# A Fourier mixing layer and a SwiGLU block on one core: value weights issued one fold earlier, row clears behind the rows, an angle counter in PSUM, Wo in longer packets

## The chip, the cores and the metric

The kernel runs on 1 core of one Trainium2 chip. The metric is device time in microseconds. Five engines take part: TensorE (PE, with its weight loads as PEld), VectorE (DVE), ScalarE (ACT), GpSimd (POOL) and SyncE (SP). SP issues nothing but DMAs; ACT and POOL issue some too, between their instructions. Each engine runs its instructions in the order in which they stand, and waits on semaphores for the others.

## The reference

```
def _attn_ref(x):                      # x: 8 x 3008 x 256, f32
    X = np.fft.fft(x, axis=1)
    X = np.fft.fft(X, axis=2)
    return X.real
def _moe_ref(x, w_gate, w_val, w_out): # x: 24064 x 256, d_ff = 1536
    g = x @ w_gate
    silu = g * (1.0 / (1.0 + np.exp(-g)))
    val = x @ w_val
    return silu * val @ w_out
```

The second takes the first's output as its rows. All inputs and the output are f32.

## The kernel before

**What is computed how.** The Fourier transform along 256 is folded into the gate and value weights: they are multiplied by tables of cosines (`CD`) and sines (`SDt`) once and give `Wp`, `Wq` and `Wm` (`Wq` with mirrored signs), three bf16 tiles of 128 rows, for gate and value (`gv`) 1536 columns each. The transform along 3008 is done by symmetry: rows of x are folded into sums and differences (on POOL, `fold_steps`), and tables `Tab` of cosines and sines times these give `Pt` (from the cosines) and `Qt` (from the sines), 512 columns of outputs a tile, for a plus and a mirrored minus half. For each tile and each of 12 chunks of d_ff, PE multiplies `Wp` with `Pt` and `Wq` or `Wm` with `Qt` (line 1086), ACT takes the silu (1167, 1199, 1210), DVE or POOL multiply by the value half (1191, 1217, 1187, 1230) and give `hp` and `hm`, and PE multiplies these with `Wo` (1257). Chunk f of d_ff is the columns f*128 to f*128+127 of the weights and row block f of `Wo`.

**Two parts.** The prologue (to line 748) is written out by hand: batch 0's rows, the tables, the first weights. What comes after stands in an order that a planner (`Sched`, line 860) makes from estimated costs and a table of shifts while the program is built; it also gives each product a PSUM bank (`bank`, line 1090). Its order is fixed in the program; nothing is decided on the chip.

**The prologue's steps around the change.** x is loaded into `XA` (128 rows by 8 blocks; batch 0's first rows) and `XC0` (the rest of batch 0) by `rise_c`, `fall_a` and `fall_c` on the queues of SP and ACT. `place` (line 471) brings rows into the order of others by a product with a 0/1 matrix and leaves the result in PSUM: `psA` for XA, `psC` for XC0. DVE adds and subtracts (`sums`, 485, into `SA` and `SC`; `direct`, 582, into `SBc`). `fold_d` (537) folds `SA` on POOL (539) and ACT casts it to bf16 (540). PE multiplies the folded rows (`half_folded`, 527) and the unfolded ones (`unfolded`, 534) with `Tab` into four PSUM tiles `acc[eo][q]`; ACT copies one half out (685), DVE adds the other (690) into `Pt` and `Qt`. `load_w(fc)` (423) issues the loads of 512 weight columns on POOL's DMA queue, with a cast from f32 to bf16: `fc` 0 into `W0`, 1 and 2 into parts of `XA` that are free by then. `half_w` (504) multiplies `W0` with `CD` and `SDt`, ACT copies the result (511) into `Wp` and `Wq`.

**Odd angles.** The cosines and sines for odd rows are made later: `turns` (396, on POOL, row 398) multiplies a counter `kfO`, 376 columns of 1, 5, 9, ..., by two columns `mM` and rounds to whole turns; `angles` (400, on DVE, row 402) multiplies the counter again and subtracts the turns; ACT takes the magnitude (1471) and the sine and cosine (409, 412). Counter, turns and angles all lie in `XA`. `angle_op(ch)` puts these into the planner's list for `ch` 0 and 1 at two units.

**Weights 512 to 1535** are transformed in the planner's part (`weight_op`, 1433): products at 1442, ACT's copies at 1445, 1448 and 1451.

**Row clears.** `load_c(1)` loads batch 1's remaining rows into partitions 64 to 123 of `XC` and one more row into partition 124. The rows that no load fills are cleared by two DMAs of zeros of 64 KB, `clear_rest` (317): one from a zero part of `XC0`, one from a part of `Af` that POOL sets to zero at line 604.

Of the kernel before, what the change touches and what calls it, by code (L numbers as in the profile page):

```python
# [12 lines left out]
F32 = mybir.dt.float32  # L13
I32 = mybir.dt.int32
BF16 = mybir.dt.bfloat16
AF = mybir.ActivationFunctionType
# [48 lines left out]
def kernel(  # L65
# [8 lines left out]
    nc = tc.nc  # L74
    B, M, D = x.shape
    Dff = moe_w_gate.shape[1]
    P = 128
    H = M // 2
    G = M // 8
# [3 lines left out]
    T = 512  # L83
# [15 lines left out]
    NCR = GH - P  # L99
# [37 lines left out]
    Wg = const.tile([P, 1, Dff], BF16, name="Wg")  # L137
    Wo = const.tile([P, nF, D], BF16, name="Wo")
    Tab = const.tile([P, 2, 2, 2, NTAB], BF16, name="Tab")
    halfpi = const.tile([P, 1], F32, name="halfpi")  # L140
    zero = const.tile([P, 1], F32, name="zero")
    w0 = const.tile([P, 2, nF], F32, name="w0")
    sel = const.tile([P, P], BF16, name="sel")
    CD = const.tile([P, 2, P], BF16, name="CD")
    SDt = const.tile([P, 2, P], BF16, name="SDt")
    m2 = const.tile([P, 1], F32, name="m2")
    mM = const.tile([P, 4], F32, name="mM")
    Z0 = const.tile([P, 2, 3, P], BF16, name="Z0")
    wC = const.tile([P, 1], F32, name="wC")
    sgn = const.tile([P, 1], F32, name="sgn")  # L150
    XA = const.tile([P, 8, 2, D], F32, name="XA")
    XC = const.tile([P, 8, 2, D], F32, name="XC")
    SDf = const.tile([P, R2 // D + 1, D], F32, name="SDf")
# [4 lines left out]
    Wraw = [XAw[:, i * 4 * T:(i + 1) * 4 * T].rearrange("p (n f) -> p n f", n=2) for i in range(2)]  # L158

    rrO = XA.rearrange("p a q d -> p (a q d)")[:, 4 * T:4 * T + 4 * G].rearrange("p (c q n) -> p c q n", c=2, q=2)  # L160
    kfO = XA.rearrange("p a q d -> p (a q d)")[:, 4 * T + 4 * G:4 * T + 5 * G]


    LA, NA = 8, P // 8
# [131 lines left out]
    def rise_c(hi, eng):  # L296
        eng.dma_start(out=XC3[64 * hi:64 * hi + 64, 0:2, :],
                      in_=rows_at(0, 2 * (P + 1) - 1 + 2 * hi * R, [[2 * D, 64], [R * D, 2], [1, 2 * D]]))

    def fall_c(hi, a, eng):  # L300
        eng.dma_start(out=XC3[64 * hi:64 * hi + NCR, 2 + a, :], in_=down_set(0, 3 - 2 * hi - a, JC, LC, NC_))
# [5 lines left out]
    fall_a(1, nc.scalar)  # L307
    fall_a(0, q)
    rise_c(0, q)
    fall_c(1, 0, nc.scalar)  # L310
    fall_c(1, 1, nc.scalar)
    rise_c(1, q)
    fall_c(0, 0, q)
    fall_c(0, 1, q)
    X3c = XC.rearrange("p a q d -> p (a q d)")

    def clear_rest(hi, zeros):
        q.dma_start(out=X3c[64 * hi + NCR:64 * hi + 64, :].rearrange("p (c d) -> p c d", d=D),
                    in_=zeros[64 * hi + NCR:64 * hi + 64].unsqueeze(1).to_broadcast([64 - NCR, 16, D]))

    clear_rest(0, xf[:, 7 * D:8 * D])

    iota = dict(channel_multiplier=0, allow_small_or_imprecise_dtypes=True)
    pcol = tp.tile([P, 1], F32, name="pcol")
# [59 lines left out]
    nc.vector.memset(EOf[:, 1, :, P:P + 1], 0.0)  # L384
    vts(m2, pcol, scalar1=0.0, scalar2=-2.0, op0=Alu.not_equal, op1=Alu.mult)
    vts(sgn, half, scalar1=1.0 / 32, scalar2=1.0, op0=Alu.mult, op1=Alu.add)
    sgo = const.tile([P, 1], F32, name="sgo")
    vts(sgo, pc, scalar1=float(NCR), scalar2=-2.0, op0=Alu.is_equal, op1=Alu.mult)
    vts(sgo, sgo, scalar1=1.0, scalar2=sgn, op0=Alu.add, op1=Alu.mult)
    vts(wC, pc, scalar1=float(LC - 1), scalar2=-0.5, op0=Alu.is_equal, op1=Alu.mult)  # L390
# [47 lines left out]
    nc.gpsimd.dma_start(out=XC0[NCR:64 + NCR + 1:64, 2:4, 0],  # L438
                        in_=rows_at(0, 0, [[2 * R * D, 2], [R * D, 2], [1, D]]))
    more_iotas()  # L440


    ce_angle = [[tp.tile([P, 2, NCE], F32, name=f"{nm}{ch}") for nm in ("rr", "ra")] for ch in range(2)]
    tp.tile([P, 1900], F32, name="pad")
# [59 lines left out]
    def half_w(h, k, pool, nm):  # L504
        ps = pool.tile([P, 2, T // 2], F32, name=nm)
        dst, tab = ((Wp, CD), (Wq, SDt))[k]
        fs = slice(h * T // 2, (h + 1) * T // 2)
        for gv in range(2):
            for no in range(2):
                nc.tensor.matmul(ps[:, gv, :], tab[:, no, :], W0[gv][:, no, fs], start=(no == 0), stop=(no == 1))  # L510
        nc.scalar.copy(dst[:, :, fs], ps)

    def start_acc(eo):
        for q, (pool, nm) in enumerate(((psV, "v"), (psG, "g"))):
            acc[eo][q] = pool.tile([P, T], F32, name=nm)
# [79 lines left out]
    sums(SA, 1, XA, psA)  # L595
    start_acc(0)
    half_folded(0, 0)
    half_folded(0, 2)
    psC = place(XC0, putC, 2, ((psG, "g"), (psV, "v")))
    start_acc(1)  # L600
    fold_d(1, 0)
    half_folded(1, 0)
    zeros = Af.rearrange("p a b d -> p (a b d)")[:, 0:D]
    nc.gpsimd.memset(zeros, 0.0)
    clear_rest(1, zeros)
    load_w(0, (1,))
    d_tables()
    fold_d(1, 2)
    direct(0)
    direct(1)  # L610
    first_columns()
# [97 lines left out]
    first_tile = {(b, part): tile_of(b * H + part * 2 * G) for b, part in jobs}  # L709
    unfolded(0, SBc)  # L710
    transform(0, 0, (0,), acc)
    sums(SC, 0, XC0, psC)
    half_folded(1, 2)
    load_w(1)
    nc.gpsimd.iota(kfO, pattern=[[4, G]], base=1, **iota)
    heads(nc.gpsimd, hc[:, 0], hc[:, 1], CEc)
    turns(rrO[:, 0].bitcast(I32), kfO, 0)
    load_w(2)
# [12 lines left out]
    for h in range(2):  # L731
        fs = slice(h * T // 2, (h + 1) * T // 2)
        nc.scalar.activation(Wm[:, :, fs], Wq[:, :, fs], AF.Copy, scale=m2)
    nc.gpsimd.dma_start(out=Wo, in_=moe_w_out.rearrange("(f p) d -> p f d", p=P))
    for q in range(2):
        quarter_rows(ptt, EOA[:, 0, :, q, :], EOA[:, 1, :, q, :], BBa[:, q])

# [350 lines left out]
    S = Sched()  # L1088

    def bank(k):  # L1090
        return PS[:, S.place[k[0]], :]

    def work(k):
        return singles[S.place[k[0]]]
# [331 lines left out]
    for b, part in jobs[1:]:  # L1426
        for eo in range(2):
# [2 lines left out]
                u += 1  # L1430
            job_at[u] = (b, part, eo)

    def weight_op(fc, gv):
        for k in range(2):
            ko = (("B", "w", (fc, gv, k)), 0)
            dst, tab = ((Wp, CD), (Wq, SDt))[k]
            src = Wraw[gv][:, :, (fc - 1) * T:fc * T]
            fs = slice(fc * T, (fc + 1) * T)

            def product(ko=ko, tab=tab, src=src):  # L1440
                for no in range(2):
                    nc.tensor.matmul(bank(ko), tab[:, no, :], src[:, no, :], start=(no == 0), stop=(no == 1))

            def even(ko=ko, dst=dst, fs=fs):
                nc.scalar.copy(dst[:, gv, fs], bank(ko))  # L1445

            def odd(ko=ko, dst=dst, fs=fs):
                nc.scalar.copy(dst[:, gv, fs], bank(ko))

            def mirrored(ko=ko, fs=fs):  # L1450
                nc.scalar.activation(Wm[:, gv, fs], bank(ko), AF.Copy, scale=m2)

            def mirrored_pool(dst=dst, fs=fs):
                pts(Wm[:, gv, fs], dst[:, gv, fs], scalar1=m2, scalar2=1.0, op0=Alu.mult, op1=Alu.mult)

            S.add("PE", 2 * pe_us(T), product, r=[(("W",), (fc, gv)), (("A",), "preW")], w=[ko], new=[ko[0]], cat="pe", bits=(0, T))
            if k:
                S.add("ACT", act_us(T), odd, r=[ko], w=[(("Wq",), (fc, gv))])
                if (fc, gv) in WM_ACT:
                    S.add("ACT", act_us(T) + 0.1, mirrored, r=[ko], w=[(("Wm",), (fc, gv))])  # L1460
# [5 lines left out]
    raO = SDf.rearrange("p a d -> p (a d)")[:, 0:4 * G].rearrange("p (c q n) -> p c q n", c=2, q=2)  # L1466

    def angle_op(ch):
        S.add("DVE", 1.6, lambda: angles(rrO[:, ch], kfO, ch, rrO[:, ch].bitcast(I32)),
              r=[(("A",), "pre")], w=[(("rr",), ch)])  # L1470
        S.add("ACT", 0.72, lambda: nc.scalar.activation(raO[:, ch], rrO[:, ch], AF.Abs), r=[(("rr",), ch), (("A",), "pre")],  # L1471
              w=[(("ra",), ch), (("fold",), "F")])
# [84 lines left out]
    for i, u in enumerate(units):  # L1557
# [1 line left out]
        for op in before.pop(i, ()):  # L1559
            op()  # L1560
        if i == 1:
            loads.extend((("C", 1), k, fn) for k, fn in enumerate(load_c(1, nc.sync)))
        if i == 8:
            loads[0:0] = [(("A", 1), k, fn) for k, fn in enumerate(load_a(1, nc.sync))]
        run_loads(LOADS)
# [79 lines left out]
```

## Time and profile before

| what | us |
|---|---|
| median of 3 runs | 607.62 (607.51 to 607.91) |
| the profiled execution, its own time | 608.29 |
| its span in the profile | 606.5 |
| PE busy | 595.2 |
| ACT busy | 566.6 |
| DVE busy | 565.4 |
| POOL busy | 547.4 |

How to read the rows below. A row of the timeline has start and duration in us, engine, line, operation, output<-inputs with shapes, how many instructions are merged, and in brackets the idle time before and what ended it. `SPq`, `ACTq` are an engine's sequencer issuing DMAs. A row of the chain of waits has start, duration and what the end was waiting for then; `issue` is time in which an engine waited for nothing that the profile shows. A row of the stretches has from:to, its length, the busy time of PE, PEld, DVE, ACT and POOL with counts, the granted clock, the DMA share and GB/s. A row of a group has the line, engine, operation and shape, the count, busy us, mean ns of one, and idle time before. A DMA row has the count, KB each and the median us from issue to landing; a queue row has packets, MB and the share of 16 DMA engines.

### The profile page before, as it was taken

Reading aid. Unit: us, or ns where it says so; the run is one execution under the profiler, and the core shown is the slowest. Engines: PE = TensorE matmul, PEld = TensorE weight load, DVE = VectorE, ACT = ScalarE, POOL = GpSimd, SP = SyncE. Lnnn points to the kernel's source line nnn. Section 1 sums busy time; section 2 is a strip of 40 time slices with the busy share of each in tenths; the row PEclk is TensorE's granted clock in tenths of the full one; section 3 lists DMA queues with packets and bytes.
Section 4 is the critical chain, followed back from the end, with each engine's and each line's share of the span. In section 5 each row is a group of like instructions: output and inputs, shape, how many; then the busy total and the mean of one; then the engine's idle time right before and its main releaser. Section 6 shows DMA issues by size and latency. Waiting matters only on the chain.

```text
span 606.5 us, 12721 instructions
## 1 busy us (share of the span) xinstructions
PE 595.2 (98%) x4058; PEld 393.1 (65%) x4058; DVE 565.4 (93%) x1050; ACT 566.6 (93%) x1101; POOL 547.4 (90%) x507
## 2 busy tenths in 40 slices
PE   8799999999999999999999999999999999999997
PEld 5445666676666766666666666666666666666686
DVE  8868999989889999999999999999999999999993
ACT  7599899999998999999999999999999899999994
POOL 8969699999999999999998999998989889868873
PEclk9999999999999999999999999999999999999999
DMA  9943335544504623454124412227121211212112
GB/s 224 160 114 97 99 104 157 166 122 129 140 18 119 154 63 111 121 150 130 51 70 100 114 46 62 71 80 174 48 62 36 64 45 45 65 43 68 54 54 79
DMA packets 50737, 57.72 MB, mean 95 GB/s; under 512 B 7256, under 2 KB 37724, under 8 KB 50670
## 3 DMA queue, kind: packets, MB, share of 16 engines
q1 hardware_dynamic: 47016, 53.78, 32.2%
q0 software_dynamic: 3216, 2.36, 3.0%
q10 hardware_dynamic: 438, 0.77, 0.4%
q8 instruction: 32, 0.52, 0.4%
q14 instruction: 35, 0.29, 0.2%
HBM read 29.43 MB, written 24.65 MB: 89 GB/s over the span
## 4 chain that ended last, share of the span: by engine, by line
PE 92%; ACT 3%; DVE 2%; DMA 1%; issue 1%; POOL 1%; POOLq 0%; DVEq 0%
PE ps L1086 45%; PE ps L1257 41%; PE ps L1388 4%; DMA W<-in_moe_w_val_dram 1%; PE ps L648 1%; POOL EOA L539 1%; DVE XA L402 1%; DVE rr L402 0%; ACT Tab L412 0%; ACT wk5s L1199 0%; ACT Tab L1517 0%; ACT SDf L1471 0%; ACT Wp L1445 0%; PE ps L534 0%; DVE hp L1191 0%
## 5 line engine op out<-in xcount | busy, mean ns | idle before, releaser
L1086 PE MATMUL ps<-Pt,Wp 128*128 128x512 bf16 (+2 forms) x576 | 203.3, 375 | 0.7 <-ACT wk1s L1199 0.2
L1257 PE MATMUL ps<-Wo,hm 128*128 128x256 bf16 (+2 forms) x1140 | 164.3, 273 | 0.0
L1257 PE MATMUL ps<-Wo,hp 128*128 128x256 bf16 (+2 forms) x1140 | 162.7, 273 | 0.0
L1086 PE MATMUL ps<-Qt,Wq 128*128 128x512 bf16 (+2 forms) x440 | 160.0, 375 | 0.0
L1257 PEld LDWEIGHTS <-hm 128*128 128x128 bf16 (+2 forms) x1140 | 111.8, 98 | 58.2 <-issue 1.0
L1257 PEld LDWEIGHTS <-hp 128*128 128x128 bf16 (+2 forms) x1140 | 111.9, 98 | 53.1 <-PE ps L1086 0.3
L1230 POOL TENSOR_TENSOR hm<-sv0q 128x1024 bf16<-128x1024 f32 (+2 forms) x68 | 126.6, 1862 | 14.9 <-ACT sv0q L1199 10.8
L1230 POOL TENSOR_TENSOR hm<-sv1q 128x1024 bf16<-128x1024 f32 (+2 forms) x66 | 122.8, 1861 | 9.0 <-DVE sv1q L1223 3.9
L1086 PE MATMUL ps<-Qt,Wm 128*128 128x512 bf16 (+2 forms) x286 | 102.1, 376 | 2.3 <-DVE hp L1191 2.2
L1142 ACT ACTIVATE ps<-bc,w 128x512 f32<-128x512 bf16 (+2 forms) x136 | 95.5, 716 | 0.5
L1086 PEld LDWEIGHTS <-Wp 128*128 128x128 bf16 x576 | 56.2, 98 | 29.1 <-issue 1.3
L1086 PEld LDWEIGHTS <-Wq 128*128 128x128 bf16 x440 | 43.0, 98 | 28.6 <-issue 4.6
L1199 ACT ACTIVATE sv0q<-ps 128x512 f32<-128x512 f32 (+1 forms) x87 | 57.4, 671 | 2.8 <-PE ps L1086 1.9
L1199 ACT ACTIVATE sv1q<-ps 128x512 f32<-128x512 f32 (+1 forms) x85 | 55.7, 669 | 2.0 <-POOL hm L1230 1.2
L1086 PEld LDWEIGHTS <-Wm 128*128 128x128 bf16 x286 | 27.9, 98 | 15.3 <-issue 0.8
L207 POOL TENSOR_TENSOR SDf<-XA 128x1020 f32<-128x1020 f32 x14 | 33.0, 2357 | 1.1 <-DMA XC<-in_x_dram 1.1
L217 POOL TENSOR_TENSOR Af<-EOf 128x516 f32<-128x516 f32 (+1 forms) x22 | 24.2, 1099 | 0.4
L214 POOL TENSOR_TENSOR EOf<-SDf 128x512 f32<-128x512 f32 (+1 forms) x22 | 24.0, 1090 | 0.0
L211 POOL TENSOR_TENSOR EOf<-SDf 128x512 f32<-128x512 f32 (+1 forms) x22 | 24.0, 1090 | 0.0
L1152 DVE SCALAR_TENSOR_TENSOR wk10s<-bc,w,ps 128x512 f32<-128x512 bf16 (+2 forms) x32 | 23.1, 722 | 0.2 <-PE ps L1086 0.2
L1086 PE MATMUL ps<-Qt,Wg 128*128 128x512 bf16 (+2 forms) x61 | 22.6, 371 | 0.0
L1388 PE MATMUL ps<-Tab,St 128*128 128x376 bf16 (+1 forms) x64 | 20.0, 323 | 0.0
(448 smaller groups left out, 1414.3 us busy)
## 6 DMA issues: line engine op xcount, KB each, us to landing
XA<-in_x_dram SPq DMA_DIRECT2D x30, 256.0 KB
XA<-in_x_dram SPq DMA_DIRECT2D x112, 64.0 KB
XC<-in_x_dram SPq DMA_DIRECT2D x30, 120.0 KB
XC<-in_x_dram SPq DMA_DIRECT2D x105, 32.0 KB
bc<-br SPq DMA_DIRECT2D x21, 128.0 KB
out_dram<-wk0s SPq DMA_DIRECT2D x19, 128.0 KB
St<-Fc SPq DMA_DIRECT2D x14, 128.5 KB
out_dram<-wk7s SPq DMA_DIRECT2D x13, 128.0 KB
```

Source lines behind the costliest of these rows:

```text
L207: tt(F[:, :, 1:D], up[:, :, 1:D], down[:, :, D - 1:0:-1], op=Alu.add)
L211: tt(E[:, :, 0:P], F[:, :, P:0:-1], F[:, :, P:D], op=Alu.add)
L214: tt(O[:, :, 0:P], F[:, :, P:0:-1], F[:, :, P:D], op=Alu.subtract)
L217: tt(Af[r], EOf[r, :, 0:2, :], EOf[r, :, 2:4, :], op=Alu.add)
L402: vstt(rr[:, i, :], kf, mM[:, 2 * ch + i:2 * ch + i + 1], t1[:, i, :], op0=Alu.mult, op1=Alu.subtract)
L1086: nc.tensor.matmul(ps[:, :n], Wt[:, gv, fs], src[:, :n], start=start, stop=stop, skip_group_check=True)
L1142: nc.scalar.activation(bank(k)[:, :self.wp], bc[self.t][:, :self.wp], AF.Copy, scale=w0[:, gv, self.f:self.f + 1])
L1152: nc.vector.scalar_tensor_tensor(work(e)[:, :self.wp], bc[self.t][:, :self.wp], w0[:, gv, self.f:self.f + 1], bank(k)[:, :self.wp], op0=Al ...
L1199: return lambda: nc.scalar.activation(self.silu(self.sm, w), src()[:, :w], AF.Silu)
L1230: lambda: nc.gpsimd.tensor_tensor(tiles_of(t)[1][:, f - 1:f + 1, :w], pair(self.vm)[:, :, :w, 1], pair(self.vm)[:, :, :w, 0], op=Alu.mult),
L1257: nc.tensor.matmul(bank(ko)[:n, j * D:(j + 1) * D], hts[t][minus][:, f, c:c + n], Wo[:, f, :], start=(f == 0), stop=(f == nF - 1))
L1388: nc.tensor.matmul(ps[:, cols], l, r_, start=(i == 0), stop=(i == len(mms) - 1), skip_group_check=True)
```

## The change

- `load_w(0, (1,))`, the value half of the first weights, is issued on POOL ahead of `fold_d(1, 0)` instead of behind it and the memset of the zeros; `d_tables` and `fold_d(1, 2)` follow, then the memset.
- `psC` is placed ahead of the second `half_folded(0, 2)`. The load `rise_c(1)` goes from SP's queue to ACT's, `fall_c(1, 1)` from ACT's to SP's.
- Both clears are taken out of the prologue. They read zeros from `Af` and stand in SP's list behind batch 1's row loads and ahead of the one more row (partition 124), which now waits for them.
- `kfO` lies in `XC` and is made by POOL behind `more_iotas`. ACT copies it to a PSUM tile that it has just emptied (`acc[0][0]`), as `kfP`, and DVE's four `angles` instructions read it there. All four stand at `angle_op(0)`'s place, ahead of the first `hp`; `angle_op(1)` issues none. `turns` on POOL still reads `kfO`. Two banks change places in `bank`, so that the planner's early products stay off that tile.
- `Wo` is loaded with two neighbouring rows of 256 a partition, so that a packet has 1 KB in place of 512 B. Row block f of `Wo` then holds every second row of a block of 256, and the weights' columns are put into the same order where ACT copies them out of PSUM: in each block of 256, column 2q+j goes to j*128+q. These copies read every second column.
- The small columns `halfpi`, `zero`, `m2`, `wC`, `sgn`, `sgo` and `mM` share one tile.

```diff
-    halfpi = const.tile([P, 1], F32, name="halfpi")
-    zero = const.tile([P, 1], F32, name="zero")
+    cols = const.tile([P, 10], F32, name="cols")
+    halfpi, zero, m2, wC, sgn, sgo = (cols[:, i:i + 1] for i in range(6))
+    mM = cols[:, 6:10]
...
-    kfO = XA.rearrange("p a q d -> p (a q d)")[:, 4 * T + 4 * G:4 * T + 5 * G]
+    kfO = XC.rearrange("p a q d -> p (a q d)")[:, 4 * T:4 * T + G]
...
     rise_c(0, q)
+    rise_c(1, nc.scalar)
     fall_c(1, 0, nc.scalar)
-    fall_c(1, 1, nc.scalar)
-    rise_c(1, q)
+    fall_c(1, 1, q)
...
-    def clear_rest(hi, zeros):
-        q.dma_start(out=X3c[64 * hi + NCR:64 * hi + 64, :].rearrange("p (c d) -> p c d", d=D),
-                    in_=zeros[64 * hi + NCR:64 * hi + 64].unsqueeze(1).to_broadcast([64 - NCR, 16, D]))
-
-    clear_rest(0, xf[:, 7 * D:8 * D])
+    def clear_rest(hi, zeros, r0):
+        n = zeros.shape[0]
+        nc.sync.dma_start(out=X3c[64 * hi + NCR + r0:64 * hi + NCR + r0 + n, :].rearrange("p (c d) -> p c d", d=D),
+                    in_=zeros.unsqueeze(1).to_broadcast([n, 16, D]))
...
     more_iotas()
-
+    nc.gpsimd.iota(kfO, pattern=[[4, G]], base=1, **iota)
...
-        nc.scalar.copy(dst[:, :, fs], ps)
+        nc.scalar.copy(dst[:, :, fs].rearrange("p g (j q) -> p g j q", j=2), ps.rearrange("p g (q j) -> p g j q", j=2))
...
     half_folded(0, 0)
+    psC = place(XC0, putC, 2, ((psG, "g"), (psV, "v")))
     half_folded(0, 2)
-    psC = place(XC0, putC, 2, ((psG, "g"), (psV, "v")))
     start_acc(1)
+    load_w(0, (1,))
     fold_d(1, 0)
     half_folded(1, 0)
+    d_tables()
+    fold_d(1, 2)
     zeros = Af.rearrange("p a b d -> p (a b d)")[:, 0:D]
     nc.gpsimd.memset(zeros, 0.0)
-    clear_rest(1, zeros)
-    load_w(0, (1,))
-    d_tables()
-    fold_d(1, 2)
...
     transform(0, 0, (0,), acc)
+    kfP = acc[0][0][:, 0:G]
+    nc.scalar.copy(kfP, kfO)
...
-    nc.gpsimd.iota(kfO, pattern=[[4, G]], base=1, **iota)
...
-    nc.gpsimd.dma_start(out=Wo, in_=moe_w_out.rearrange("(f p) d -> p f d", p=P))
+    nc.gpsimd.dma_start(out=Wo.rearrange("p (b j) d -> p b (j d)", j=2), in_=moe_w_out.rearrange("(b p j) d -> p b (j d)", p=P, j=2))
...
-        return PS[:, S.place[k[0]], :]
+        return PS[:, (0, 1, 2, 3, 4, 6, 5, 7)[S.place[k[0]]], :]
...
+    def turned(a):
+        return a.rearrange("p (b j q) -> p b j q", b=2, j=2)
+
+    def unturned(a):
+        return a.rearrange("p (b q j) -> p b j q", b=2, j=2)
...
-                nc.scalar.copy(dst[:, gv, fs], bank(ko))
+                nc.scalar.copy(turned(dst[:, gv, fs]), unturned(bank(ko)))
...
-                nc.scalar.activation(Wm[:, gv, fs], bank(ko), AF.Copy, scale=m2)
+                nc.scalar.activation(turned(Wm[:, gv, fs]), unturned(bank(ko)), AF.Copy, scale=m2)
...
-        S.add("DVE", 1.6, lambda: angles(rrO[:, ch], kfO, ch, rrO[:, ch].bitcast(I32)),
+        S.add("DVE", 1.6, lambda: ch or [angles(rrO[:, c], kfP, c, rrO[:, c].bitcast(I32)) for c in range(2)],
...
         if i == 1:
-            loads.extend((("C", 1), k, fn) for k, fn in enumerate(load_c(1, nc.sync)))
+            steps = load_c(1, nc.sync)
+            pad_row = steps.pop()
+            steps.append(lambda: [clear_rest(1 - h, zeros[64 * (1 - h) + NCR:64 * (1 - h) + 64], 0) for h in range(2)] + [pad_row()])
+            loads.extend((("C", 1), k, fn) for k, fn in enumerate(steps))
```

More of the change, by code (lines that the diff above doesn't have):

```diff
@@ L145 @@
     SDt = const.tile([P, 2, P], BF16, name="SDt")
-    m2 = const.tile([P, 1], F32, name="m2")
-    mM = const.tile([P, 4], F32, name="mM")
     Z0 = const.tile([P, 2, 3, P], BF16, name="Z0")
-    wC = const.tile([P, 1], F32, name="wC")
-    sgn = const.tile([P, 1], F32, name="sgn")
     XA = const.tile([P, 8, 2, D], F32, name="XA")
@@ L386 @@
     vts(sgn, half, scalar1=1.0 / 32, scalar2=1.0, op0=Alu.mult, op1=Alu.add)
-    sgo = const.tile([P, 1], F32, name="sgo")
     vts(sgo, pc, scalar1=float(NCR), scalar2=-2.0, op0=Alu.is_equal, op1=Alu.mult)
@@ L1444, in even @@
             def even(ko=ko, dst=dst, fs=fs):
-                nc.scalar.copy(dst[:, gv, fs], bank(ko))
+                nc.scalar.copy(turned(dst[:, gv, fs]), unturned(bank(ko)))
             def odd(ko=ko, dst=dst, fs=fs):
-                nc.scalar.copy(dst[:, gv, fs], bank(ko))
+                nc.scalar.copy(turned(dst[:, gv, fs]), unturned(bank(ko)))
             def mirrored(ko=ko, fs=fs):
-                nc.scalar.activation(Wm[:, gv, fs], bank(ko), AF.Copy, scale=m2)
+                nc.scalar.activation(turned(Wm[:, gv, fs]), unturned(bank(ko)), AF.Copy, scale=m2)
             def mirrored_pool(dst=dst, fs=fs):
```

## The prediction

> **What bounds the kernel now.** I read the page first, then busy time by stretch, then the chain of waits in order of time, then the timeline of the stretch that the chain points to.
>
> ```profile
> PE 595.2 (98%) x4058; PEld 393.1 (65%) x4058; DVE 565.4 (93%) x1050; ACT 566.6 (93%) x1101; POOL 547.4 (90%) x507
> ```
>
> ```profile
> 20.00:24.50 4.50, 4.24 (x33) 2.82 (x33) 2.86 (x10) 2.34 (x5) 4.32 (x8) 1.00 1.11 172
> 24.50:29.50 5.00, 3.06 (x15) 1.31 (x14) 5.00 (x5) 3.36 (x7) 5.00 (x10) 1.00 1.15 173
> 29.50:43.30 13.80, 12.90 (x79) 5.65 (x78) 8.65 (x16) 13.80 (x27) 8.42 (x16) 1.00 0.52 115
> 60.00:100.00 40.00, 40.00 (x276) 26.88 (x274) 38.18 (x71) 36.48 (x71) 33.55 (x33) 1.00 0.41 110
> 100.00:594.00 494.00, 493.91 (x3383) 329.59 (x3382) 476.74 (x858) 477.29 (x934) 459.10 (x384) 1.00 0.32 88
> ```
>
> In each row of the second view stand the length, then PE, weight load, DVE, ACT and POOL busy, granted clock, DMA share. From 60 us to 594 us PE does not pause at all (40.00 of 40.00, 493.91 of 494), at full clock. Nothing in the diff alters how much work PE does there. So the end can only move if that stretch starts at another time, or if something begins to starve it. Before it lie a prologue in which engines wait for one another and, from 29.5 to 43.3, a stretch in which ACT is busy 13.80 of 13.80 and PE is not. The chain says what starts that stretch:
>
> ```profile
> 13.79 6.20 DMA W<-in_moe_w_val_dram
> ...
> 20.03 0.38 PE ps L510 x2
> 20.41 1.28 PE ps L534 x8
> 21.69 0.75 PE ps L654 x8
> 22.44 0.56 PE ps L510 x4
> ...
> 23.02 0.42 ACT Wq L511
> ...
> 24.51 2.12 DVE XA L402
> ...
> 28.67 0.83 ACT SDf L1471
> ...
> 43.28 1.23 PE ps L1086 x5
> ```
>
> Two things set the start of ACT's full stretch: PE waits for the value weights until 20.03, and ACT then waits for the odd angles on DVE (L402) until 28.67.
>
> **The change part by part. Value weights.** POOL issues them in program order, behind two folds and a memset.
>
> ```profile
> 11.45 2.14 POOL L539 TENSOR_TENSOR EOA<-SA 128x512 f32<-128x512 f32 x2
> ...
> 13.79 0.73 POOL L428 DMA_DIRECT2D W<-in_moe_w_val_dram  x1
> 13.87 0.68 SPq L318 DMA_DIRECT2D XC<-Af  x1
> 13.91 1.88 PE L476 MATMUL ps<-XC,putC 128*128 128x512 f32 x4
> ...
> 14.97 1.95 DVE L582 TENSOR_TENSOR SBc<-ps,XC 128x256 bf16<-128x256 f32 x5 [1.69 <-PE ps L476]
> ...
> 18.20 0.38 PE L510 MATMUL ps<-W,CD 128*128 128x256 bf16 x2
> ```
>
> The issue now stands behind one fold: 11.45 + 2.14/2 = 12.52 instead of 13.79, 1.27 earlier. The landing is less sure:
>
> ```profile
> q0 software_dynamic: 316, 0.31, 101.4%
> ```
>
> ```profile
> XA<-in_moe_w_gate_dram POOLq DMA_DIRECT2D x2, 256.0 KB, 4.2
> ...
> W<-in_moe_w_gate_dram POOLq DMA_DIRECT2D x1, 256.0 KB, 6.6
> W<-in_moe_w_val_dram POOLq DMA_DIRECT2D x1, 256.0 KB, 6.2
> ```
>
> The first row is POOL's queue from 14 to 17 us: its packets alone fill the 16 engines, so the value weights stand behind the gate weights there. They took 6.2 us from issue to landing, transfers of their size 4.2 when the crowd had gone. That bounds the landing between 12.52 + 4.2 = 16.7 and 12.52 + 6.2 = 18.7. I take 18.2: nearer the late end, since the gate weights still run ahead, but inside it, since the two 64 KB row clears (the L318 row is one) no longer mix in. PE must be there too. Its first pair on the gate weights ran at 18.20 behind the half-folded and unfolded products. Those shift forward, because the XC0 placement (L476) now goes ahead of the second half-fold: DVE, which idled 1.69 for it, can begin SBc near 13.4, and the price, that fold (1,0) stands 0.73 behind the issue, falls on a cast that PE reaches only after the placement. The placement needs the XC0 rows; of these the upper rising half goes from SP, where it stood second behind a wait, to ACT's queue, where it is issued sooner, and one falling set goes the other way: the same bytes, all behind the XA rows that the first sums need, so no cost there. PE can take the value pair at about 18.3: a gain of 20.03 − 18.3 = 1.7. Bounds: 0 (landing unmoved) and 2.0 (PE ready a few tenths before its 18.20). The rows from 20.41 to 23.02 are the same work in the same order and move along.
>
> **Odd angles.**
>
> ```profile
> 24.43 4.20 DVE L402 SCALAR_TENSOR_TENSOR XA<-XA,mM 128x376 f32<-128x376 f32 x2
> ...
> 25.09 0.72 POOL L229 TENSOR_TENSOR BBa<-EOA 128x256 bf16<-128x256 f32 x1
> ...
> 26.46 0.57 ACT L1167 ACTIVATE wk1s<-ps 128x480 f32<-128x480 f32 x1
> ...
> 28.55 0.64 DVE L1191 TENSOR_TENSOR hp<-wk0s,ps 128x480 bf16<-128x480 f32 x1
> 28.67 0.83 ACT L1471 ACTIVATE SDf<-XA 128x752 f32<-128x752 f32 x1 [1.64 <-DVE XA L402]
> ...
> 29.25 0.36 PE L1086 MATMUL ps<-Qt,Wm 128*128 128x480 bf16 x1 [1.83 <-DVE hp L1191]
> ...
> 29.68 1.12 DVE L402 SCALAR_TENSOR_TENSOR XA<-XA,mM 128x376 f32<-128x376 f32 x2
> ```
>
> ```profile
> L402 DVE SCALAR_TENSOR_TENSOR XA<-XA,mM x4: 598/830/3217, 24.4 to 30.2; 128x376 f32<-128x376 f32 x4
> ```
>
> Four equal instructions took 0.6 to 3.2 us; the slow pair, 4.20 together, ran while POOL did two-input folds (L229), the fast pair, 1.12, beside scalar work. With the counter in PSUM only one input is left in SBUF, and the PSUM-fed DVE rows (hp, 0.64 for 480 columns) show no such stretch. So four instructions at 1.12/2 = 0.56 make 2.24, all ahead of the first hp. Started 1.7 earlier, at 22.7, the first pair ends at 23.85. ACT ends wk1s at 27.03 − 1.7 = 25.3 and no longer waits: the 1.64 is gone whole. The price of putting all four first is that hp is two instructions later than it could be: 22.7 + 2.24 = 24.95, still 3.6 before 28.55, and PE's product behind it (29.25) follows; the silus that need that product come only after SDf and wk2s. Next on that path is ACT itself. Bounds: 0 to 1.64.
>
> **Wo, clears, counter, banks.** Taken at nothing, with their cover:
>
> ```profile
> 17.82 0.48 POOL L715 IOTA XA<- 128x376 f32 x1
> ```
>
> ```profile
> 34.36 0.64 SPq L194 DMA_DIRECT2D XC<-in_x_dram  x1
> ...
> 42.54 2.35 POOL L207 TENSOR_TENSOR SDf<-XC 64x1020 f32<-64x1020 f32 x1
> ```
>
> The iota goes into POOL's wait before its first fold, and takes 0.48 out of the row of POOL work behind 17.82. The copy of the counter to PSUM is one more ACT instruction of 376 columns (about the 0.57 of a 480-column one); it lies in ACT's wait for the value weights. The scheduled products that would have used its bank now use another, freed by ACT's last Wq copy; PE meets it on its fourth product, behind which it waits for hp anyway. The Wo packets halve in number; their first reader, the L1257 output products, stands after 43.28. The two clears now sit in SP's queue between the row loads and L194, which must wait for them to land. Behind L194 on SP stand the XA loads, behind them all the fold at 42.54: two issues of 0.68 end at 35.7, and a landing that takes from nothing to the 4.2 us above puts L194 between 35.7 and 39.9, and its own landing at most at 44.1. POOL would be ready at 42.54 − 3.3 = 39.2, so its fold is late by 0 to 4.9 against the rest; I take 1, since 64 KB out of SBUF is a small transfer. PE does not see that unless POOL's backlog lasts to where PE needs hm.
>
> **Weight copies with every second column.** Fourteen ACT copies (4 at L511, 10 at L1445 to L1451) now read PSUM with step two, in the stretch where ACT is the bound. No row here reads with step two. Nearest rows:
>
> ```profile
> L305 ACT COPY XC<-zero 128x1024 f32<-128x1024 f32 x1 | 1.0, 1027 | 0.0
> ...
> L511 ACT CAST Wp<-ps 128x512 bf16<-128x512 f32 x2 | 1.2, 589 | 2.9 <-PE ps L510 2.9
> ```
>
> ```profile
> L1199 ACT ACTIVATE sv1q<-ps 128x512 f32<-128x512 f32 x81 | 53.2, 671 | 2.0 <-POOL hm L1230 1.2 <-PE ps L1086 0.7
> L1167 ACT ACTIVATE wk0s<-ps 128x512 f32<-128x512 f32 x19 | 11.9, 627 | 0.4 <-PE ps L1086 0.4
> ```
>
> If the skipped words cost as much as read ones, a copy is a 1024-column one: 1027 − 589 = 0.44 each, 6.1 in all. A step of two on the write side costs 671 − 627 = 0.04, 0.6 in all. A gain is excluded: no fewer elements. I take 0.02 each, 0.3, close to the strided row, because ACT's rows go by elements.
>
> [...]
>
> **Sum:** −1.7 − 1.64 + 0.3 = −3.0, say −3.1 with the DVE time that the second pair no longer takes from the ACT stretch. That execution took 608.29 for a span of 606.5; against the median of 607.62 the shift gives **604.5**. Its own range, from a landing at the late end to PE's limit with free copies, is 603.2 to 605.4.
>
> **Rivals.** *The weights land no sooner*, because POOL's queue was full (101.4%). Then DVE starts at 24.43, ACT is free at 27.03, and only the 1.64 goes: 607.62 − 1.64 + 0.3 = 606.3. Against it: part of the traffic in that crowd was moved away. *Slower: the step of two in PSUM.* At 0.44 each, 6.1 − 3.3 = +2.8, 610.4; it decides from 3.3/14 = 0.24 per copy, that is copies of 0.83 us in place of 0.59. For it: ACT is full there, so every one counts. *The gain is given back by POOL*, whose fold waits for the clears and the row behind them: 1 to 2 us of 3.1, so 604.5 + 1.5 = 606.0. Against it: POOL has 6.4 us free between 60 and 100. *PSUM does not free the angles*: the turns they subtract are still in SBUF. Then all four stand ahead of hp, 22.7 + 4.2 + 1.1 = 28.0 against 28.55, and the shift is about 0.5: 607.1.
>
> [...]
>
> **How the numbers follow.** Forecast 0.64; weights no sooner 0.13; step of two 0.10; given back 0.07; angles not freed 0.06. About 0.2% (1.2 us) is what a measurement of this kernel tells from no change. The forecast, the given-back case and most of the 606.3 case are faster: 0.80; the angles and the rest 0.10; the step of two 0.10. The range takes in the forecast, its bounds below and the two cases near 606: 602.8 to 606.5.
>
> **What would show it.** The value pair on L510 near 18.3; four angle rows of 0.56 ending near 25 with hp behind them; no wait ahead of L1471, near 25.6; the PE row of 43.28 near 40; L511 and L1445 unchanged at 0.6. Copies of 0.8 or more, or a PE share below full after 60 us, would make it wrong.

## The result, and the profile after

| | before | after |
|---|---|---|
| median, us | 607.81 (607.51 to 608.79, 6 runs) | 604.21 (603.28 to 605.22, 6 runs) |
| the profiled execution, its own time | 608.29 | 603.9 |
| its span | 606.5 | 601.9 |

The ratio of after to before is 0.9939, with a 95% interval of 0.9926 to 0.9951: 3.6 us faster. The forecast was 604.5. Line numbers after are 4 smaller in the prologue than before (402 is now 398, 511 is 507, 1086 is 1082) and 2 larger in the weight part (1445 is 1447, 1471 is 1473).

The page's first part, and the busy time by stretch, of the kernel after:

```profile
PE 595.1 (99%) x4058; PEld 393.1 (65%) x4058; DVE 562.7 (93%) x1050; ACT 567.4 (94%) x1102; POOL 546.0 (91%) x507
```

```profile
24.50:29.50 5.00, 5.00 (x25) 2.19 (x23) 3.26 (x6) 5.00 (x11) 4.91 (x12) 1.00 1.04 182
29.50:43.30 13.80, 12.90 (x82) 6.02 (x81) 8.98 (x15) 13.80 (x27) 9.40 (x16) 1.00 0.38 88
60.00:100.00 40.00, 39.74 (x277) 26.93 (x275) 38.27 (x71) 36.56 (x71) 37.13 (x35) 1.00 0.47 129
```

PE does the same work (595.1 against 595.2). From 24.5 to 29.5 PE and ACT are now busy 5.00 of 5.00; before they had 3.06 and 3.36. ACT's full stretch begins there and no longer at 28.67. From 60 to 100 PE is no longer full: 39.74 of 40. The chain of waits of after, in order of time, and its timeline:

```profile
15.86 1.28 PE ps L530 x8
...
17.82 0.44 PE ps L506 x4
...
24.88 0.72 ACT SDf L1473
...
39.36 1.23 PE ps L1082 x5
```

```profile
12.49 0.72 POOL L424 DMA_DIRECT2D W<-in_moe_w_val_dram  x1
...
17.66 0.60 PE L506 MATMUL ps<-W,CD 128*128 128x256 bf16 x4
...
22.28 2.15 DVE L398 SCALAR_TENSOR_TENSOR XA<-ps,cols,XA 128x376 f32<-128x376 f32 x4
...
24.45 0.66 DVE L1187 TENSOR_TENSOR hp<-wk0s,ps 128x480 bf16<-128x480 f32 x1
...
24.76 0.84 ACT L1473 ACTIVATE SDf<-XA 128x752 f32<-128x752 f32 x1
```

Gate and value products run in one piece, 17.66 to 18.26, where before the value pair alone ended at 20.41: 2.15 earlier, 1.7 forecast. The chain of waits reaches them through PE's products on `SBc` (L530) and not through a DMA. The four angles take 2.15, 0.54 each, and are done before hp. ACT starts SDf at 24.76 with no wait in brackets, 3.9 before its 28.67, and the PE row that stood at 43.28 stands at 39.36: 3.92 earlier. Not all of that reaches the end. The last output products (28 of L1257, now L1253) start at 595.11 against 598.96, 3.85 earlier. The spans of these two executions differ by more, 4.6, because of how the execution of before ended: from the start of ACT's last full copy to SP's issue of its result it took 1.65 us, and 0.61 in after. (The first rows are of before, the others of after.)

```profile
598.96 3.34 PE L1257 MATMUL ps<-Wo,hm 128*128 128x256 bf16 x28
...
600.96 0.58 ACT L1263 COPY wk0s<-ps 128x512 f32<-128x512 f32 x1 [1.38 <-PE ps L1257]
...
602.61 0.81 SPq L1269 DMA_DIRECT2D out_dram<-wk0s  x2
```

```profile
595.11 3.34 PE L1253 MATMUL ps<-Wo,hm 128*128 128x256 bf16 x28
...
597.12 0.59 ACT L1259 COPY wk0s<-ps 128x512 f32<-128x512 f32 x1 [1.38 <-PE ps L1253]
597.73 0.81 SPq L1265 DMA_DIRECT2D out_dram<-wk0s  x2
```

That difference of a microsecond belongs to the execution, not to the change: in the profiled execution of a_clears_first below the same step took 2.11.

### The profile page after: what moved, and what is told of

Same layout as the page of the kernel before. It is cut to its first block, busy times and chain, and to the rows that moved or that the text cites. A ratio compares the mean times of both kernels' runs of the same rounds, so it can differ in the third digit from the quotient of the medians.

```text
span 601.9 us, 12720 instructions
## 1 busy us (share of the span) xinstructions
PE 595.1 (99%) x4058; PEld 393.1 (65%) x4058; DVE 562.7 (93%) x1050; ACT 567.4 (94%) x1102; POOL 546.0 (91%) x507
## 4 chain that ended last, share of the span: by engine, by line
PE 93%; ACT 3%; DVE 1%; DMA 1%; issue 1%; SPq 0%; DVEq 0%; ACTq 0%
PE ps L1082 46%; PE ps L1253 41%; PE ps L1384 4%; DMA XA<-in_x_dram 1%; PE ps L643 1%; DVE SA L481 1%; PE ps L530 0%; ACT Tab L408 0%; ACT wk5s L1195 0%; DVE SBc L578 0%; ACT Tab L1519 0%; PE ps L506 0%; PE ps L523 0%; ACT SDf L1473 0%; ACT Wp L1447 0%
## 5 line engine op out<-in xcount | busy, mean ns | idle before, releaser
L1253 PE MATMUL ps<-Wo,hm 128*128 128x256 bf16 (+2 forms) x1140 | 164.3, 273 | 0.0
L1253 PE MATMUL ps<-Wo,hp 128*128 128x256 bf16 (+2 forms) x1140 | 162.7, 273 | 0.0
L1253 PEld LDWEIGHTS <-hm 128*128 128x128 bf16 (+2 forms) x1140 | 111.8, 98 | 57.9 <-issue 0.6
L1253 PEld LDWEIGHTS <-hp 128*128 128x128 bf16 (+2 forms) x1140 | 111.9, 98 | 53.0 <-issue 0.2
L1082 PEld LDWEIGHTS <-Wp 128*128 128x128 bf16 x576 | 56.2, 98 | 29.5 <-issue 1.8
```

The lines of the kernel that those rows point to most:

```text
L1082: nc.tensor.matmul(ps[:, :n], Wt[:, gv, fs], src[:, :n], start=start, stop=stop, skip_group_check=True)
L1253: nc.tensor.matmul(bank(ko)[:n, j * D:(j + 1) * D], hts[t][minus][:, f, c:c + n], Wo[:, f, :], start=(f == 0), stop=(f == nF - 1))
```

## The experiments

The theory at this point: the start of ACT's full stretch sets the end, the value weights and the angles each move it, the step of two in PSUM is free. Rivals: the two parts are not independent; it was the order of the angles and not PSUM; it was the missing clears and not the place of issue. Ratios are to the kernel before, run on the same chip in turn.

| run | median us | ratio, 95% interval | ACT SDf starts | PE row of 43.28 | PE busy, 60 to 100 |
|---|---|---|---|---|---|
| before | 607.81 | 1 | 28.67 | 43.28 | 40.00 |
| after | 604.21 | 0.9939 (0.9926 to 0.9951) | 24.76 | 39.36 | 39.74 |
| b_value | 608.0 | 0.9988 (0.997 to 1.0006) | 25.50 | 40.12 | 40.00 |
| b_value_again | 609.05 | 0.9998 (0.998 to 1.0016) | 28.67 | 44.55 | 39.94 |
| b_angles | 606.3 | 0.9961 (0.9947 to 0.9975) | 27.00 | 41.63 | 40.00 |
| a_sbuf_angles | 605.68 | 0.995 (0.9936 to 0.9964) | 24.78 | 41.13 | 39.73 |
| a_straight | 604.37 | 0.9927 (0.9911 to 0.9943) | 24.76 | 39.38 | 38.87 |
| a_value_late | 603.48 | 0.9915 (0.99 to 0.993) | 24.51 | 39.13 | 40.00 |
| a_value_earlier | 604.54 | 0.9935 (0.9915 to 0.9955) | 24.94 | 39.55 | 38.70 |
| a_order_back | 604.43 | 0.9937 (0.9924 to 0.9951) | 25.30 | 39.90 | 39.30 |
| a_clears_back | 604.45 | 0.9942 (0.9928 to 0.9955) | 25.05 | 39.66 | 39.79 * |
| a_clears_first | 603.22 | 0.9914 (0.9901 to 0.9928) | 24.76 | 39.37 | 40.00 |
| a_both | 603.21 | 0.9917 (0.9904 to 0.9931) | 24.64 | | 39.79 * |
| after_again | 603.95 | 0.9929 (0.9917 to 0.9942) | 24.76 | 39.38 | 39.79 * |

\* The same 39.79 in all three, and no wait of PE from 60 to 100 us in any of them. Their matmul records there (278 in a_both and after_again, 277 in a_clears_back) are fewer than their weight loads (280 in each), where a_clears_first at 40.00 has 282 and 280: some matmul records are missing from these traces. From a_order_back some are missing too (270 and 273); PE's waits in it from 43 to 601 us come to 0.5.

**b_value: the value weights alone, from before.**

```
     half_folded(0, 0)
+    psC = place(XC0, putC, 2, ((psG, "g"), (psV, "v")))
     half_folded(0, 2)
-    psC = place(XC0, putC, 2, ((psG, "g"), (psV, "v")))
     start_acc(1)
+    load_w(0, (1,))
     fold_d(1, 0)
...
     clear_rest(1, zeros)
-    load_w(0, (1,))
```

> The kernel before, with only two moves: the value weights issued ahead of fold (1,0) and the memset, and the XC0 placement ahead of the second half-fold. The row clears stay in the prologue, the odd angles still read their counter from SBUF, two before hp and two after. Theory (the start of ACT's full stretch sets the end; this part is worth what the value pair on L510 gains, after showed it at about 18.0 in place of 20.03): the issue near 12.5; landing 5.2 to 6.2 later, at 17.7 to 18.7; pair at 18.0 to 18.8; ACT's wait ahead of SDf (L1471) stays at about 1.6; time 607.8 - 1.6 = 606.2 (605.6 to 606.6). Rival (it was the removal of the clears from the crowd, not the place of issue, that made the weights land sooner): landing at 18.7 or later, pair at 19 or later, 606.8 to 607.8.

Neither. The median is that of before, yet two of the 12 executions took 604.5, and the one profiled was one of them. In it the value pair ran at 18.61, the first angles began at 23.02, and ACT started SDf at 25.50 without a wait, so that this part alone brought the PE row 3.16 forward:

```profile
18.61 0.38 PE L510 MATMUL ps<-W,CD 128*128 128x256 bf16 x2 [0.43 <-DMA W<-in_moe_w_val_dram]
...
23.02 1.73 DVE L402 SCALAR_TENSOR_TENSOR XA<-XA,mM 128x376 f32<-128x376 f32 x2
...
26.32 2.06 DVE L402 SCALAR_TENSOR_TENSOR XA<-XA,mM 128x376 f32<-128x376 f32 x2
```

So a second trace was taken.

**b_value_again: the same kernel.**

> The same kernel as b_value, for a second trace: of its 12 runs two took 604.5 and ten 607.6 to 610.2, and the one profiled was a short one, in which the first angle pair ran at 23.02 in 1.73, half of it before POOL began its folds, so that hp came at 25.19 and SDf at 25.50. Theory (most executions lose the whole gain again on DVE: with SBUF inputs the first angle pair overlaps POOL's folds for longer as soon as it starts a little later): value pair at 18.6 to 20, first angle pair 4 or more, hp near 28 or later, PE's full stretch starting where it does in the kernel before; time 607.5 to 608.5. Rival (the landing varies: in the long executions the value pair stands at 20 as before, and the angles play no part): pair at 20 or later, 607.5 to 608.5. A third trace like the first, 604.5, would leave it open.

A long execution, and its first angle pair took over 4 us, as the theory said. But the value pair stood at 19.77, close to the rival's 20: the landing varied too, by more than a microsecond between these two executions. The angle instructions by line, with the shortest, median and longest in ns, in the short execution and in the long one; then the long one's timeline:

```profile
L402 DVE SCALAR_TENSOR_TENSOR XA<-XA,mM x4: 715/1052/1128, 23.0 to 27.3; 128x376 f32<-128x376 f32 x4
```

```profile
L402 DVE SCALAR_TENSOR_TENSOR XA<-XA,mM x4: 596/831/3470, 24.2 to 30.2; 128x376 f32<-128x376 f32 x4
```

```profile
19.77 0.38 PE L510 MATMUL ps<-W,CD 128*128 128x256 bf16 x2 [0.79 <-DMA W<-in_moe_w_val_dram]
...
24.18 4.45 DVE L402 SCALAR_TENSOR_TENSOR XA<-XA,mM 128x376 f32<-128x376 f32 x2
...
27.21 0.93 POOL L742 TENSOR_TENSOR EOf<-SC 128x256 f32<-128x256 f32 x1
28.13 1.08 POOL L746 TENSOR_SCALAR St<-EOf,sgn 128x128 bf16<-128x128 f32 x2
28.56 0.64 DVE L1191 TENSOR_TENSOR hp<-wk0s,ps 128x480 bf16<-128x480 f32 x1
28.67 0.83 ACT L1471 ACTIVATE SDf<-XA 128x752 f32<-128x752 f32 x1 [1.89 <-DVE XA L402]
```

Begun 0.25 earlier than before (24.18 for 24.43), the pair took 0.25 longer (4.45 for 4.20), and hp stands at 28.56 where before had 28.55. The slow instruction is the first of the pair, and in both traces it ends at 27.65 (24.18 + 3.47, and 24.43 + 3.22 before), amid POOL's two-input folds, which run from 23.56 to 28.14. The fold in which it ends, L742, took 0.93; the same fold took 0.63 in b_angles, with the counter in PSUM. So in these two traces the loss looks like a hold to a fixed time and not like a price for each instruction, and it takes back what came sooner ahead of it. The times fit: none of the 20 executions of this kernel lies between 604.7 and 607.5.

What sets the hold is not shown. In the short execution the first pair began at 23.02, before POOL's folds at 23.59; but its second pair began at 26.32, amid them, and was not held either: all four got by with 0.72 to 1.13. In the traced long execution most was lost before the hold: against the short one the value pair was 1.16 late at its landing, and only 0.25 of gain was left for the hold to take. With the clears still in the prologue, the value weights alone are worth nothing in 17 of these 20 executions, and over 3 us in the others. No run has them with the clears gone and the angles as before.

**b_angles: the angles alone, from before** (the banks 5 and 6 exchanged as in after).

```
     nc.gpsimd.iota(kfO, pattern=[[4, G]], base=1, **iota)
+    kfP = acc[0][0][:, 0:G]
+    nc.scalar.copy(kfP, kfO)
...
-        S.add("DVE", 1.6, lambda: angles(rrO[:, ch], kfO, ch, ...),
+        S.add("DVE", 1.6, lambda: ch or [angles(rrO[:, c], kfP, c, ...) for c in range(2)],
```

> The kernel before, with only the odd angles changed: counter copied to PSUM, all four angle instructions ahead of the first hp, scheduled products' banks 5 and 6 exchanged. Theory: four rows of 0.54 in the place of two of 2.1, beginning near 24.4 and ending near 26.6, ACT's SDf without the wait of 1.64, hp near 26.7, the PE row of 43.28 near 41.6; time 607.8 - 1.7 = 606.1 (605.8 to 606.4). Rival (the two parts of the change only gain together, because the weights' landing still sets the start): within 0.5 of before, 607.3 to 607.8.

A hit: four angles in 2.15, SDf at 27.00 without a wait, the PE row at 41.63, 1.65 before 43.28.

**a_sbuf_angles: after, the angles read the counter from SBUF** (`kfO` for `kfP`, nothing else).

> The kernel after, with the four angle instructions in the same place but reading the counter from SBUF (where it stands in XC) instead of its copy in PSUM. Theory (two SBUF inputs on DVE lose time while POOL runs folds with two inputs; the PSUM copy is what frees them): of the four some take 2 to 3 us beside POOL's folds, together 4.5 to 8 in place of 2.15, hp later by 2.5 to 5, time 604.2 + 1 to 3 = 605.2 to 607.2. Rival (the order, four together and earlier, did it): four rows of about 0.55, time 604.2 +- 0.5.

The time is inside the theory's range, the rows differ from it: all four are slowed alike, none to 3 us.

```profile
L398 DVE SCALAR_TENSOR_TENSOR XA<-XC,cols,XA x4: 1035/1070/1222, 22.3 to 25.4; 128x376 f32<-128x376 f32 x4
```

In after the same view has 601 ns for each. The four end to end take 4.17 for 2.15, which makes hp late by 1.94 (26.39 for 24.45) and the PE row by 1.77. The order alone does not give the 2.15; taking one input out of SBUF does.

**a_straight: after, Wo in 512-byte packets and no step in the copies** (the three `rearrange` pairs taken out).

> The kernel after, with the output weights loaded in 512-byte packets as before and all 14 weight copies reading PSUM and writing without a step. Theory (a step of two in PSUM costs ACT nothing that the end sees): L507 rows 0.59 as in after, time 604.2 +- 0.6. The forecast's own term of 0.02 each: 603.9. [...]

The copies of both kernels, by line (L507 of after, then of a_straight; L1447 of after, then of a_straight):

```profile
L507 ACT CAST Wp<-ps x2: 585/588/592, 18.3 to 21.4; 128x512 bf16<-128x512 f32 x2
...
L1447 ACT CAST Wp<-ps x4: 610/690/750, 26.4 to 35.1; 128x512 bf16<-128x512 f32 x4
```

```profile
L507 ACT CAST Wp<-ps x2: 586/588/591, 18.3 to 21.4; 128x512 bf16<-128x512 f32 x2
...
L1447 ACT CAST Wp<-ps x4: 608/690/752, 26.4 to 35.1; 128x512 bf16<-128x512 f32 x4
```

588 and 588, 690 and 690: ACT's copies pay nothing for the step, where the upper estimate of the prediction had 0.44 each. The Wo part is worth nothing that these runs can tell.

**a_value_late and a_value_earlier: after, the value weights issued behind fold (1,0) again, or right behind the gate weights.**

```
-    load_w(0, (1,))
     fold_d(1, 0)
     half_folded(1, 0)
+    load_w(0, (1,))
```

> The kernel after, with the value weights issued behind fold (1,0) again, all else as in after (no clears in the prologue, placement first). Theory (both the place of issue and the missing clears make them land sooner; b_value, with the clears, landed 6.1 after its issue and the pair ran at 18.61, after at 5.2 and 17.96): issue near 13.6, landing 4.7 to 5.2 later at 18.3 to 18.8, pair 0.4 to 0.9 later than in after, four angles and hp later by as much; time 604.2 + 0.4 to 0.9 = 604.6 to 605.1. Rival (only the place of issue counts): pair at 20.0, 606.2. Rival (only the clears' absence counts, the queue was the limit): pair at 18.0, 604.2.

> The kernel after, with the value weights issued right behind the gate weights, ahead of folds (0,2) and (1,0). Theory (in after the chain of waits runs through the x loads, DVE's sums, SBc and PE's products in front of the value pair, and no longer through the weights' landing: PE is now the one that comes last): pair at 18.0 as in after, time 604.2 +- 0.4. Rival (the pair still stands at its landing, 17.65): pair up to 0.3 sooner, 603.9. Rival on the slow side (an issue of 0.73 on POOL ahead of fold (0,2) makes EOA's half and the half-folded products late): the L523 products and the pair 0.5 to 0.7 later, 604.8.

**a_order_back and a_clears_back: only the clears out of the way, or all but the clears.** The first is a_value_late with the XC0 rows' queues and the placement as before. The second is after with both clears in the prologue again.

```
-    rise_c(1, nc.scalar)
     fall_c(1, 0, nc.scalar)
-    fall_c(1, 1, q)
+    fall_c(1, 1, nc.scalar)
+    rise_c(1, q)
...
+    clear_rest(0, xf[NCR:64, 7 * D:8 * D], 0)
...
+    clear_rest(1, zeros[64 + NCR:128], 0)
```

> The kernel after, with the value weights behind fold (1,0), the XC0 rows shared out over SP's and ACT's queues as before, and the XC0 placement behind the second half-fold as before: of the whole change at the value weights only the missing row clears are left. Theory (the clears are what makes the landing slow: 6.1 to 7.2 in before, b_value and b_angles, which have them, 4.0 to 5.8 in all that have not): landing 4.0 to 4.6, at 17.6 to 18.2; value pair by 18.0 to 18.9, since the placement and SBc are later; time 603.5 to 604.8. Rival (the queues of the XC0 rows did it): landing at 6 or more, pair near 20, 605.5 to 606.3.

> The kernel after, with the two row clears in the prologue as before (for that the counter stands in XA again, made behind load_w(1), so the copy to PSUM waits for it, to about 18.8); value weights early, rows and placement as in after. Theory (the clears): landing 6.1 to 7.2 after an issue near 12.5, pair at 18.6 to 19.8, angles from PSUM at 0.54 each, time 604.9 to 606.0. Rival (rows, placement and place of issue): landing 5.2, pair at 18.0, 604.2 to 604.7 with the 0.5 of the later counter.

The four together, by the DMA view (the last number is us from issue to landing): after, a_value_late, a_order_back, a_clears_back.

```profile
W<-in_moe_w_val_dram POOLq DMA_DIRECT2D x1, 256.0 KB, 5.2
```

```profile
W<-in_moe_w_val_dram POOLq DMA_DIRECT2D x1, 256.0 KB, 4.0
```

```profile
W<-in_moe_w_val_dram POOLq DMA_DIRECT2D x1, 256.0 KB, 4.3
```

```profile
W<-in_moe_w_val_dram POOLq DMA_DIRECT2D x1, 256.0 KB, 5.6
```

Issue plus landing: 17.7, 17.5, 17.8, 18.1. Issued a microsecond later, the weights land no later, as long as the clears are gone, and a_order_back shows that their absence is enough by itself. With the clears there and the late issue (before, b_angles) it is 20.0 and 20.1. The early issue by itself is no such cure: with the clears there it gave 18.6 and 19.7 in the two traces of b_value's kernel, and 18.1 in a_clears_back, where the XC0 rows' queues are exchanged as well; how much of that is the queues and how much is chance, one trace cannot tell. In all nine traces without clears in the prologue the landing is at 17.2 to 17.8, in the five with them at 18.1 to 20.1. Of the theory for a_value_late nothing is left; its second rival held. a_value_earlier came as its theory said (the pair from 17.83, 604.54): a still earlier issue brings nothing.

a_value_late has the earliest ACT start of all, because the early issue has a price. It takes POOL 0.72 ahead of fold (1,0), ACT casts that fold half a microsecond later, and PE waits 0.50 for it. (The profile puts this wait down to DVE; but these products read `EOb`, whose cast ends at 15.00, and in a_value_late, where DVE is no earlier, there is no wait.) First after, then a_value_late:

```profile
14.38 0.62 ACT L536 CAST EOb<-EOA 128x512 bf16<-128x512 f32 x1 [0.42 <-POOL EOA L535]
...
15.05 0.82 PE L523 MATMUL ps<-Tab,EOb 128*128 128x377 bf16 x4 [0.50 <-DVE SBc L578]
```

```profile
13.84 1.48 PE L523 MATMUL ps<-Tab,EOb 128*128 128x377 bf16 x8
13.85 0.59 ACT L536 CAST EOb<-EOA 128x512 bf16<-128x512 f32 x1
```

PE's first pair on the weights runs at 17.11 there, for 17.66 in after. What a_order_back lacks against a_value_late, 0.79 at ACT's start, is the placement (L472 at 13.91 there, at 12.05 with the new order): with the weights there in time, PE's own products come last.

**a_clears_first: after, the clears ahead of SP's row loads.**

```
-            steps.append(lambda: [clear_rest(1 - h, ...) for h in range(2)] + [pad_row()])
+            steps.append(pad_row)
+            first_row = steps[0]
+            steps[0] = lambda: [clear_rest(1 - h, ...) for h in range(2)] + [first_row()]
```

> The kernel after, with the two row clears on SP ahead of the first of the 20 row loads (after: behind the last but one, ahead of the pad row L191, which has to wait for them to land). Theory (SP stands still from 36.2 to 39.5 in after, 36.3 to 40.6 in a_straight, because the pad row waits for the clears; that makes POOL's fold L204 wait 1.2 to 2.3, and PE lost 0.26 and 1.13 between 60 and 100 in those two runs): the pad row and the XA loads 3 to 5 earlier, near 35 and 36; POOL's fold without a wait for the clears; PE busy 40.00 of 40.00 from 60 to 100; the shift of the start stays whole; time 604.2 - 0.3 to 1.1 = 603.1 to 603.9. Rival (POOL's backlog after 43 has other causes, for a_sbuf_angles lost 0.27 there with its fold waiting for ACT and not for the clears): PE still 39.7 there, time 604.2 +- 0.3. Rival on the slow side (1.5 to 2 us of SP ahead of the row loads make the rows, and the fold of C, later by that much): fold L204 later than in after, 604.5 or more.

SP's and POOL's rows in after, then in a_clears_first:

```profile
34.11 2.08 SPq L316 DMA_DIRECT2D XC<-Af  x2
39.51 0.65 SPq L191 DMA_DIRECT2D XC<-in_x_dram  x1
40.39 7.11 SPq L178 DMA_DIRECT2D XA<-in_x_dram  x14
...
54.23 0.61 SPq L1544 DMA_DIRECT2D bc<-br  x1
...
61.92 2.35 POOL L204 TENSOR_TENSOR SDf<-XA 128x1020 f32<-128x1020 f32 x1 [5.33 <-DMA XC<-in_x_dram]
```

```profile
22.14 1.50 SPq L316 DMA_DIRECT2D XC<-Af  x2
...
38.18 0.65 SPq L191 DMA_DIRECT2D XC<-in_x_dram  x1
39.07 5.86 SPq L178 DMA_DIRECT2D XA<-in_x_dram  x14
...
49.63 0.62 SPq L1544 DMA_DIRECT2D bc<-br  x1
...
57.45 2.36 POOL L204 TENSOR_TENSOR SDf<-XA 128x1020 f32<-128x1020 f32 x1
```

In after the pad row waits until 39.51 for clears whose issue ended at 36.19. The XA loads come only 1.3 earlier without that wait, not 3 to 5 as expected, as two issues now stand ahead of the rows; but SP's bc<-br comes 4.6 earlier, and POOL's first fold of XA no longer waits 5.33. Most of the 4.6 is a second wait: in after SP stands 4.2 us for br to land, in a_clears_first 1.1. It stood 3.9 to 4.6 in the five traces that left PE short, and at most 2.8 in the others with the clears behind; why br lands late is not shown. PE is full from 60 to 100. Of the seven traces with the clears behind the rows, five left PE short there by 0.26 to 1.30 (after, a_straight, a_sbuf_angles, a_value_earlier, a_order_back); after_again and a_value_late were full, and so were a_clears_first and a_both. Whether an execution stalls is thus partly chance with the clears behind; with them in front it was not seen, but in two traces only.

**after_again and a_both: after on the same chip as the last runs, and the two best edits together** (a_value_late's and a_clears_first's).

> The kernel after, unchanged, on the same chip as the three others of this set, to compare them with. Every theory: ratio to before 0.994 (0.9926 to 0.9951 the first time), 604.2 to 604.6; PE between 60 and 100 short of full by 0 to 1.3, as in after (0.26) and its close relatives (a_straight 1.13, a_value_earlier 1.30), where SP's bc<-br came at 54 to 56.

> The kernel after, with the value weights issued behind fold (1,0) again (as in a_value_late) and the two row clears ahead of SP's row loads (as in a_clears_first). Theory (the first takes 0.2 off the start of ACT's full stretch, the second keeps SP's br and bc rows early and PE full after 60): PE row of 39.36 near 39.13, bc<-br near 49.6, PE 40.00 from 60 to 100, time 0.8 to 1.3 below after_again, some 603.0. Rival (the two gains are one and the same, that of PE after 60): as a_clears_first and a_value_late by themselves, 603.2 to 603.5.

a_both gains 0.74 on after_again by the medians, less than the theory's 0.8 to 1.3 and no more than either edit alone: the rival is closer. after_again itself, at 603.95, lies a little below the 604.2 to 604.6 that was expected. The intervals of the ratios overlap, so a better version is likely, not proven. The traces' last output products start at 594.41 (a_both) and 594.56 (after_again), against 595.11 in after. As the trace of after_again is one in which PE did not run short, these two cannot say how much of the 0.74 is PE's.

## Why the prediction was right, point by point

- **What bounds it.** Right. The PE row moved by 3.92, and with PE nearly full after it (39.74 of 40) the last products moved by 3.85; in after_again, with PE not short and the same PE row within 0.02, they moved by 4.40.
- **Odd angles, 1.64.** Right in mechanism and size: 1.65 by b_angles. The forecast took the loss on DVE as a price of each instruction; in the traces of before and b_value_again it looks like a hold to 27.65, whenever the instruction began, so that there the angles' part is what lets an earlier gain count. In after the last three of the four lie beside POOL's folds too (from 22.96 on), and each of the four takes 0.60; with both inputs in SBUF the pairs that overlapped these folds took 0.72 to 3.47 an instruction in before and in the two traces of b_value's kernel, and the four of a_sbuf_angles 1.04 to 1.22.
- **Value weights, 1.7.** The size was near, 2.15 in after, but the step "the issue now stands behind one fold" is not its cause. The prediction sized the landing by the place of issue and gave the clears a part only as traffic. The runs showed that the clears decide, though not how they delay the landing: without them the weights land at 17.5 to 17.8 even from the late issue, and then PE's order (the placement) is what counts. The price of the early issue, said to fall "on a cast that PE reaches only after the placement", was paid by PE: 0.50. And the 1.7 and 1.64 were added as if they were independent. They are not: in the short execution of b_value's kernel ACT's start moved by 3.17 without the angles' part, in the long one not at all.
- **Steps in PSUM, +0.3.** Mis-sized by all of it: 0.00 by a_straight (588 and 690 ns with the step and without). The rival of 610.4 is out.
- **Clears, taken at nothing.** The prediction had POOL's fold late by 1, unseen by PE. It waited 1.16 for them, near that size; but what stands on SP behind the pad row was late with it, the first fold of XA waited 5.33, and PE came short in five of seven traces, by 0.26 to 1.30. This is the rival of the gain given back by POOL, in part. It offset the free copies and the larger value gain, and so the sum came within 0.3 of the median: that it came so close is luck.
- **Its own range, 603.2 to 605.4.** This does not come out of the terms given for it. A landing at 18.7 makes 607.62 − 1.33 − 1.64 + 0.3 = 604.95, and PE's limit with free copies 607.62 − 2.0 − 1.64 = 603.98.
- **Weights no sooner, angles not freed.** Both out, by the rows at 17.66 and 22.28.

## What to carry to other kernels

Before adding up gains ahead of one point, look whether something there ends at the same time however early it begins: a gain in front of such a hold is worth nothing until the hold is gone (here an instruction begun 0.25 sooner ended at the same 27.65). When a transfer lands late, take other traffic out of its way and move its issue in separate runs: here the first was enough (17.8 in a_order_back for 20.0 in before), and the second cost another engine 0.50. And a small DMA moved "out of the way" into a queue with a wait behind it is paid by what stands after that wait (here the XA loads stood at 40.39, for 39.07 with the clears in front); put it where it has long landed when it is needed.

## What the runs showed of the hardware that was not expected

A short pause of PE went with a lower clock in one trace and not in another. In b_value_again PE waited 2.1 us for hp, as before's did (1.83), and was then granted a clock of 0.58, 0.50, 0.50 and 0.71 in the four microseconds from 30; in the trace of before it was 1.00 in each. Stretches of b_value_again:

```profile
27.50:29.20 1.70, 0.00 (x0) 0.00 (x0) 1.70 (x4) 0.53 (x1) 1.70 (x3) 1.00 1.67 164
...
31.00:32.00 1.00, 1.00 (x4) 0.36 (x3) 1.00 (x3) 0.37 (x1) 1.00 (x2) 0.50 0.33 70
32.00:33.00 1.00, 1.00 (x4) 0.40 (x3) 0.51 (x1) 0.82 (x2) 1.00 (x4) 0.50 0.32 68
```

It put the PE row at 44.55 for 43.28, 1.27 later. 14 of 43 executions of before in these runs had a mean granted clock of 0.997 or less (median 608.9, the others 608.0), and 10 of 20 of b_value; of the 54 executions of the kernels with all four angles ahead of hp, none. So the change seems also to take away a chance of losing about a microsecond, which the forecast had not counted. It would explain why b_angles is 2.24 below the before of its own set (606.3 for 608.54), though its PE row moved by 1.65. That the lower mean clocks come from this pause is shown in one trace only, and a_sbuf_angles, whose PE waited 1.81 for hp, had none in 5 executions.

What stays open: why a two-input DVE instruction beside POOL's folds takes 1.04 to 1.22 in a_sbuf_angles, 0.72 to 1.13 in b_value, and up to 3.47 in before and b_value_again.
